# Dilated attention and a SiLU layer pair: dummy matmuls in TensorE's idle slots of the first batch, and a new order of the work

## The chip, the cores and the metric

The kernel runs on one core of a Trainium2 chip. The metric is the device time of one execution in microseconds; lower is better. The median of 13 runs of the kernel before is 312.4 us, from 310.62 to 316.19.

## The reference

Eight batches of eight heads, 576 positions of 64 numbers. In heads 0 to 3 a query sees the 32 positions up to its own; in heads 4 to 7 every fourth position of the last 128. The result of all heads, 512 numbers for each of 4608 tokens, goes through two matrix products with SiLU between them.

```python
scores = scale * np.matmul(q, k.transpose(0, 1, 3, 2))
mask_plain = (rel >= 0) & (rel < window)                                # window = 32
mask_dil = (rel >= 0) & (rel < window * dilation) & (rel % dilation == 0)   # dilation = 4
attn = np.exp(scores - max); attn = attn / (np.sum(attn) + 1e-09)
x = np.matmul(attn, v)            # to (tokens, 512)
h = x @ w_in                      # 512 x 2048
out = (h * (1.0 / (1.0 + np.exp(-h)))) @ w_out    # 2048 x 512
```

## The kernel before, in words

**Attention, per batch.** Plain heads are worked in six blocks of 96 queries (P steps), dilated heads by residue r modulo 4 in two halves of 72 queries (D steps, half ab). A score unit (S, L605) multiplies keys and queries of 64 rows each in two halves of the array (L632); ACT takes the exponential (L641, L645) and DVE multiplies by a mask (L650). In batch 0 the mask is added on TensorE instead by a matmul with the identity (L620). P and D steps multiply the probabilities by v with a column of ones (av, L677), and DVE divides by the sum (L680, L681) into oP or oD.

**Ways of q and k.** Batches 0 to 2 are loaded by POOL's queue into `nat` and transposed on TensorE: TD for dilated heads (L544, L557), TA and TB for plain heads (L521, L535, L582), TS and TR for the last rows of batch 0 (L594, L567). For batches 1 and 2 the N steps first pair the heads by copies (L652). Batches 3 to 7 are cast into DRAM by POOL's queue (`kq_s`, L141) and brought back by SP's transposing DMAs: two windows of the plain heads (L155), two of the dilated heads (L158).

**Ways of the result.** For batches 0 to 2 it is transposed on TensorE into xA (XP, L722; XD, L733). For batches 3 to 7 it is stored to DRAM in four parts, two of oP (L696) and two of oD (L715), and a transposing DMA (L450) brings each token group back as xA or xR when the four parts are stored.

**The two products.** Tokens are in ten groups: 256, 256 and then eight of 512, numbered 0 to 9. For each of 16 slices of 128 of the inner width, layer 1 (L892) makes h from x and w_in in four matmuls; ACT takes tanh (L901), DVE forms gT (L903). Layer 2 (L925) runs gT against w_out into y, in quarters of four matmuls; ACT copies y out and issues the store (L938, L939). Group 4 needs batch 3, group 5 batch 4, group 6 batch 5, group 7 batch 6.

**What sets the order.** The lists `order` (L743 to L767) give the sequence of a batch's steps, and a planner in Python (L280, L980 to L1037) merges them with the slices of layers 1 and 2 when the program is built. It keeps a clock of TensorE and the fill of ACT and DVE, gives each step a cost and a due time (`AT_DIL`, `AT_PLAIN` and the like are planned landings of loads), looks at the first LOOK attention steps and takes the first candidate that is ready and whose engines' backlog is under its limit. [...] PSUM banks are rings: h 2, y 1, s one of two banks, x 1, z 2; batch 0's small tiles may use x, z, h and y (L778).

**Loads.** POOL's queue issues q, k and v of batch 0 first (L205 to L209), then what ORDER (L56) lists: k0, r0 and v0 are the rest of batch 0, w0a to w3 parts of w_in, d1, p1, r1 and v1 dilated and plain q and k, raw v and shifted v of batch 1, o0 to o3 quarters of w_out. Batch 2 follows. The loads of batch b of 5 and more (`loads_gen`, L424) stand in POOL's queue behind small copies (`fence`, L427, L429) that wait for earlier transposing DMAs: of the batch before and of the group that needs batch b - 2.

**The start.** DVE clears a tile `warm` (L189, a part of vraw of batch 1) and eight matmuls of 512 columns from it into the y bank (L192) precede the first load's landing.

The planner's core, at the point that the change touches:

```python
        if pick is None:
            waits += [plan.heap[0][0]] if plan.heap else []
            plan.t = max(plan.t + 0.01, min(waits))
            continue
```

Of the kernel before, what the change touches and what calls it, by code (L numbers as in the profile page):

```python
# [16 lines left out]
def kernel(  # L17
# [35 lines left out]
    XR = 3  # L53
    NA = GA * GT
    BIG = 32768.0
    ORDER = "k0 r0 w0b v0 w0a w1 w2 w3 d1 p1 o0 r1 o1 o2 o3 v1".split()  # L56
    LOAD_US = {"w": 2.57, "o": 2.57, "d": 3.2, "p": 3.0, "r": 2.3, "v": 2.57, "k0": 2.2, "r0": 1.0, "v0": 2.3, "w0a": 1.3, "w0b": 1.3}
    AT_W0 = 11.4
    BIASED = (0,)

    cpool = ctx.enter_context(tc.tile_pool(name="const", bufs=1))
# [123 lines left out]
            )  # L185

    v_head = xRs[2][:, 0, : 2 * HN * D].bitcast(F32).rearrange("p (h d) -> p h d", h=HN)
    warm = vraws[1].rearrange("p a h r d -> p (a h r d)")
    nc.vector.memset(warm[:, :GT], 0.0)  # L189
    y_warm = ps_y.tile([P, GT], F32, tag="y", name="y_warm")  # L190
    for n in range(8):
        nc.tensor.matmul(y_warm, warm[:, :P], warm[:, :GT], start=True, stop=True)  # L192
    nc.vector.memset(warm[:, GT:], 0.0)
    nc.vector.memset(vraws[0], 0.0)
    nc.vector.memset(v_head[:W], 0.0)
    nc.vector.memset(ident_w[:, :W], 0.0)
# [161 lines left out]

    plan = Plan()
    t2 = at  # L360
    AT_DIL = {0: 6.1, 1: AT["d1"], 2: t2 + 7.0}
    AT_PLAIN = {0: 9.3, 1: AT["p1"], 2: t2 + 7.0}
    AT_VRAW = {0: 10.1, 1: AT["r1"], 2: t2 + 8.6}
    AT_VP = {0: 11.4, 1: AT["v1"], 2: t2 + 11.4}
    AT_CAST = t2 + 18.0
    AT_REST = AT["k0"]
    AT_V1 = AT["r0"]
    AT_VP1 = AT["v0"]
# [97 lines left out]
    def attention(b):  # L466
# [274 lines left out]

        if b == 0:
            order = [  # L743
                ("TA", 1, "q"), ("TA", 0, "q"), ("V", 0), ("TD", 3), ("TS", 1), ("TS", 0),
                ("TD", 0), ("TA", 0, "k"), ("TD", 2), ("TD", 1), ("TA", 1, "k"), ("S", 3),
                ("TR",), ("S", 4), ("S", 6), ("S", 0), ("S", 1), ("D", 0, 1), ("P", 1), ("S", 5),
                ("D", 0, 0), ("D", 0, 2), ("V", 1), ("P", 0), ("S", 2), ("P", 3), ("P", 2),
                ("D", 1, 1), ("P", 4), ("D", 0, 3), ("P", 5), ("XP", 0), ("XP", 1), ("D", 1, 2),
                ("XD", 0), ("D", 1, 0), ("XP", 4), ("D", 1, 3), ("XP", 5), ("XP", 2), ("XD", 1),
                ("XP", 3), ("M",), ("B",),  # L750
            ]
        elif pe_path:
            order = [
                ("N", "k"), ("TD", 3), ("TD", 0), ("TD", 2), ("V", 0), ("TD", 1), ("N", "rest"),
                ("TA", 1), ("N", "q"), ("S", 3), ("TA", 0), ("TB", 0), ("TB", 1), ("D", 0, 1),
                ("D", 0, 0), ("S", 4), ("D", 0, 2), ("S", 0), ("P", 1), ("S", 1), ("D", 0, 3),
                ("P", 2), ("P", 0), ("XP", 0), ("XP", 1), ("S", 5), ("S", 6), ("XD", 0), ("V", 1),
                ("D", 1, 3), ("XP", 2), ("S", 2), ("D", 1, 2), ("D", 1, 0), ("D", 1, 1), ("P", 3),
                ("XP", 3), ("P", 4), ("XD", 1), ("P", 5), ("XP", 4), ("XP", 5),
            ]  # L760
        else:
            order = [
                ("S", 2), ("S", 0), ("P", 1), ("S", 3), ("S", 4), ("S", 1), ("S", 5), ("P", 0),
                ("V", 0), ("P", 5), ("P", 3), ("D", 0, 3), ("V", 1), ("P", 4), ("P", 2),
                ("D", 1, 1), ("D", 1, 3), ("D", 0, 1), ("D", 0, 2), ("D", 1, 2), ("D", 1, 0),
                ("D", 0, 0),
            ]  # L767
            if pe_x:
                order.insert(order.index(("D", 0, 0)), ("XP", 0))
                order.insert(order.index(("D", 0, 0)), ("XP", 1))  # L770
                order.insert(order.index(("D", 0, 2)), ("XP", 2))
                order.insert(order.index(("D", 0, 2)), ("XP", 3))
                order.insert(order.index(("D", 1, 0)), ("XP", 4))
                order.insert(order.index(("D", 1, 0)), ("XP", 5))
                order += [("XD", 0), ("XD", 1)]
        for key in order:
# [3 lines left out]
            if kind == "N":  # L780
                st = Step(lambda ring, a=a: paired(*a), 0.0, (), [AT_PLAIN[b]], ("DVE",))
            elif kind == "B":
                st = Step(lambda ring: third_batch(), 0.0, (), [steps["XD", 1]], ())
            elif kind == "M":
                st = Step(lambda ring: masks_of(), 0.0, (), [steps["XD", 1]], ("DVE",))
            elif kind == "TA" and b == 0:
                st = Step(
                    lambda ring, a=a: trans_a0(ring, *a), 0.36, rings,
                    [AT_PLAIN[0]],
                )  # L790
            elif kind == "TD" and b == 0:
                st = Step(lambda ring, a=a: trans_d0(ring, *a), 0.17, rings, [AT_DIL[b]])
            elif kind == "TR":
                st = Step(lambda ring: trans_d1(ring), 0.34, rings, [AT_REST])
            elif kind == "TS":
                st = Step(lambda ring, a=a: trans_a1(ring, *a), 0.36, rings, [AT_REST])
            elif kind == "TA":
                st = Step(
                    lambda ring, a=a: trans_a(ring, *a), 0.36, rings,
                    [steps["N", "k"], steps["N", "rest"]], ("ACT",),  # L800
                )
            elif kind == "TB":
                st = Step(
                    lambda ring, a=a: trans_b(ring, *a), 0.18, rings, [steps["N", "q"]], ("ACT",)
                )
            elif kind == "TD":
                st = Step(lambda ring, a=a: trans_d(ring, *a), 0.28, rings, [AT_DIL[b]], ("DVE",))
            elif kind == "S":
                if not pe_path:
                    deps = [turned[b]]  # L810
                elif b == 0:
                    plain = [("TA", hp, nm) for hp in range(HP // 2) for nm in "kq"]
                    rest = [("TS", hp) for hp in range(HP // 2)]
                    dil = [("TD", h) for h in range(HN)]
                    keys = (plain, plain, plain + rest, dil, dil, dil + [("TR",)], dil + [("TR",)])
                    deps = [steps[key_] for key_ in keys[a[0]]]
                elif a[0] < 3:
                    deps = [steps[t, hp] for t in ("TA", "TB") for hp in range(HP // 2)]
                else:
                    deps = [steps["TD", h] for h in range(HN)]  # L820
                st = Step(
                    lambda ring, a=a: scores(ring, *a), 0.17 + 0.32 * (b in BIASED), ["s"] + (["hh"] if b < 2 else []),
                    deps + readers.get(base + a[0] - NP, []), ("ACT",) if b in BIASED else ("ACT", "DVE"),
                )
            elif kind == "V":
                st = Step(lambda ring, a=a: vd_of(*a), 0.0, (), [AT_V1 if b == 0 and a[0] else at_vraw], ())
            elif kind == "P":
                us = sorted({home["p", a[0], hp][0] for hp in range(HP // 2)})
                st = Step(
                    lambda ring, a=a: av_p(ring, *a), 0.13, rings,  # L830
                    [AT_VP1 if b == 0 and a[0] > 2 else at_vp] + [steps["S", u] for u in us],
                    ("DVE",),
                )
            elif kind == "D":
                us = sorted({home["d", a[0], a[1] // 2, h][0] for h in range(HN)})
                st = Step(
                    lambda ring, a=a: av_d(ring, *a), 0.13, rings,
                    [steps["V", a[0]]] + [steps["S", u] for u in us], ("DVE",),
                )
            elif kind == "XP":  # L840
                st = Step(lambda ring, a=a: x_p(ring, *a), 0.1, rings, [steps["P", a[0]]], x_eng)
            else:
                st = Step(
                    lambda ring, a=a: x_d(ring, *a), 0.28, rings,
                    [steps["D", a[0], r] for r in range(DIL)], x_eng,
                )
# [131 lines left out]
        l2 += [(g, st) for st in layer2(g, l1s_of[g])]  # L978

    plan.push(Step(None, 0.0), first_cast(), 0.0)  # L980
    LOOK = 8
    LIM_ATT = 1.1
    LIM_PAIR = 0.4
    LIM_L1 = 1.8
    SIDE = 0.9
    NEAR = 1.0
    SPARE = 6
    seconds = {st.mate for _, st in att if st.mate}
    side = 0.0
    while att or l1 or l2:  # L990
# [31 lines left out]
        if pick is None and g2 < SPARE and l2[0][1].rings and plan.backlog(l2[0][1].uses) <= 9.0:  # L1022
            l2[0][1].rings = ["y", "x", "z"]
            r = plan.ready(l2[0][1])
            if r is not None and r <= plan.t:
                pick = l2, l2[0]
        if pick is None:
            waits += [plan.heap[0][0]] if plan.heap else []
            plan.t = max(plan.t + 0.01, min(waits))
            continue  # L1030
# [37 lines left out]
```

The softmax here doesn't subtract the row's maximum and nothing guards it: scores larger than these inputs give would overflow.

## Time and profile before

| | |
|---|---|
| median of 13 runs | 312.4 us |
| the profiled execution, its own time | 313.16 us |
| its span, first to last instruction | 311.4 us |
| TensorE (PE) busy | 300.3 us, 96% |
| VectorE (DVE), ScalarE (ACT), GpSimd (POOL) busy | 196.4, 164.7, 54.7 us |
| PE busy in the first 23 us | 18.1 us |
| first h of layer 1 starts | 22.84 us |
| last layer 2 matmuls end | 308.0 us |

PE's row is matmuls, PEld's weight loads beside them. A timeline line gives start, length, engine, line, operation, tiles and count; in brackets stands idle time before it and what ended it. A line of waits gives who waited for whom, the total, the number of times and the longest. The issue of a DMA is shown at its engine's queue (SPq, ACTq), or at POOL; the data lands later. The chain of work that ended last lies 83% on PE, 36% in each of the two layers (L892, L925). From 23 us on PE is idle for little more than 6 us, 3.4 of them at the very end.

### The profile page before, as it was taken

To read this page: it belongs to the slowest core of one execution; us is meant where nothing else is said; L and a number is where in the kernel's file an instruction comes from. 1 tells how busy PE (TensorE), PEld (TensorE's weight loads), DVE (VectorE), ACT (ScalarE), POOL (GpSimd) and SP (SyncE) were. 2 spreads that over 40 slices of the span, in tenths; PEclk is the share of its full clock that TensorE was granted. 3 is DMA by queue.
4 is the path that set the end of the run, shared out by engine and by line. 5 is a ranking of instruction groups with operands and counts; after the bars stand their busy time and mean duration, and the time that the engine had idled before them with its cause. 6 is when DMAs were issued, how large, how long until landed. Compare 5 with 4: busy or idle time off the path is not lost.

```text
span 311.4 us, 6177 instructions
## 1 busy us (share of the span) xinstructions
PE 300.3 (96%) x2402; PEld 155.9 (50%) x2402; DVE 196.4 (63%) x498; ACT 164.7 (53%) x318; POOL 54.7 (18%) x86
## 2 busy tenths in 40 slices
PE   7789989999999999999999999998999999999995
PEld 3468855555445544554445444544454444444444
DVE  6389998699868735794589357944885255455000
ACT  7478873667673626444653456434644355355111
POOL 8854724000900005000500050000000000000000
PEclk9999999999999999999999999999999999999999
DMA  8999999999999749999999999964115400000122
GB/s 105 181 201 192 175 192 208 203 197 156 147 186 224 181 124 154 214 186 203 128 213 216 201 131 213 206 156 104 53 56 129 111 36 34 34 36 0 74 94 71
DMA packets 107382, 44.55 MB, mean 143 GB/s; under 512 B 73304, under 2 KB 102872, under 8 KB 107352
## 3 DMA queue, kind: packets, MB, share of 16 engines
q0 software_dynamic: 48528, 19.86, 52.4%
q1 hardware_dynamic: 53496, 14.91, 25.0%
q10 hardware_dynamic: 5328, 9.37, 8.9%
q8 instruction: 19, 0.31, 0.4%
q14 instruction: 11, 0.09, 0.1%
HBM read 39.81 MB, written 18.28 MB: 187 GB/s over the span
## 4 chain that ended last, share of the span: by engine, by line
PE 83%; DVE 6%; DMA 5%; ACT 3%; issue 1%; POOL 1%; SPq 0%; ACTq 0%; DVEq 0%; POOLq 0%
PE y L925 36%; PE h L892 36%; PE s L632 3%; PE av_d L677 3%; DMA nat<-in_q_dram 2%; PE av_p L677 2%; DMA xR<-x_s 2%; DVE gT L903 1%; DVE oD L681 1%; DVE probs L650 1%; DMA x_s<-oD 1%; PE s L620 1%; ACT probs L641 1%; ACT ob L938 1%; ACT kqD L510 1%
## 5 line engine op out<-in xcount | busy, mean ns | idle before, releaser
L925 PE MATMUL y<-w_out,gT 128*128 128x512 f16 (+1 forms) x592 | 137.8, 373 | 0.0
L901 ACT ACTIVATE th<-h 128x512 f32<-128x512 f32 (+1 forms) x160 | 88.9, 557 | 79.4 <-PE h L892 68.0
L903 DVE SCALAR_TENSOR_TENSOR gT<-th,h 128x512 f16<-128x512 f32 (+1 forms) x160 | 99.2, 629 | 47.7 <-ACT th L901 47.2
L892 PEld LDWEIGHTS <-w_in 128*128 128x128 f16 x640 | 59.0, 97 | 53.5 <-issue 2.5
L925 PEld LDWEIGHTS <-gT 128*128 128x128 f16 x592 | 55.1, 98 | 57.5
L892 PE MATMUL h<-xR,w_in 128*128 128x512 f16 x320 | 77.6, 379 | 1.1 <-DMA xR<-x_s 1.1
L892 PE MATMUL h<-xA,w_in 128*128 128x512 f16 (+1 forms) x320 | 62.1, 336 | 0.0
L938 ACT ACTIVATE ob<-y 128x512 f32<-128x512 f32 (+1 forms) x36 | 21.3, 591 | 42.7 <-PE y L925 42.7
L641 ACT ACTIVATE probs<-s 128x768 f16<-128x768 f32 (+2 forms) x32 | 24.7, 772 | 12.5 <-PE s L632 10.8
L677 PEld LDWEIGHTS <-probs 128*128 128x128 f16 x448 | 21.9, 98 | 16.4 <-DVE probs L650 3.4
L681 DVE TENSOR_TENSOR oD<-av_d,rcps 72x256 f16<-72x256 f32 x64 | 26.9, 421 | 2.2
L650 DVE TENSOR_TENSOR probs<-probs,mask_p 128x768 f16<-128x768 f16 x21 | 11.5, 552 | 22.5 <-ACT probs L641 22.5
L681 DVE TENSOR_TENSOR oP<-av_p,rcps 96x256 f16<-96x256 f32 x48 | 20.2, 421 | 1.6
L427 POOL COPY fence<-kqT 128x1 f16<-128x1 f16 x10 | 2.0, 211 | 94.3 <-DMA kqT<-kq_s 94.3
L645 ACT ACTIVATE probs<-s 128x384 f16<-128x384 f32 (+2 forms) x38 | 17.2, 479 | 1.1 <-PE s L632 1.1
L677 PE MATMUL av_d<-vd,probs 128*128 128x65 f16 x256 | 15.4, 196 | 1.3 <-DVE oD L681 0.6
L945 DVE TENSOR_SCALAR ob<-y 128x128 f32<-128x128 f32 x1 | 0.3, 292 | 20.6 <-ACT ob L943 20.6
L680 DVE RECIPROCAL rcps<-av_d 72x4 f32<-72x4 f32 x64 | 11.0, 172 | 2.7 <-PE av_d L677 2.7
L680 DVE RECIPROCAL rcps<-av_p 96x4 f32<-96x4 f32 x48 | 8.3, 172 | 6.5 <-PE av_p L677 6.5
L677 PE MATMUL av_p<-vp,probs 128*128 128x65 f16 x192 | 12.0, 194 | 0.3
L165 POOL DMA_DIRECT2D vraw<-in_v_dram x16 | 11.0, 692 | 5.5 <-DVE rcps L680 2.2
L650 DVE TENSOR_TENSOR probs<-probs,mask_d 128x576 f16<-128x576 f16 (+1 forms) x23 | 11.6, 512 | 0.0
(93 smaller groups left out, 157.4 us busy)
## 6 DMA issues: line engine op xcount, KB each, us to landing
out_dram<-ob ACTq DMA_DIRECT2D x35, 256.0 KB, 2.8
kq_s<-in_k_dram POOLq DMA_DIRECT2D x5, 576.0 KB, 9.6
kq_s<-in_q_dram POOLq DMA_DIRECT2D x5, 576.0 KB, 12.2
vp<-in_v_dram POOLq DMA_DIRECT2D x7, 384.0 KB, 8.1
w_out<-in_moe_w_out_dram POOLq DMA_DIRECT2D x4, 512.0 KB, 11.2
vraw<-in_v_dram POOLq DMA_DIRECT2D x8, 224.0 KB, 5.3
w_in<-in_moe_w_in_dram POOLq DMA_DIRECT2D x3, 512.0 KB, 9.8
x_s<-oP SPq DMA_DIRECT2D x10, 144.0 KB, 3.1
```

Source lines behind the costliest of these rows:

```text
L165: nc.gpsimd.dma_start(out=vraw[p0 : p0 + m1 - m0, ab].rearrange("p h r d -> p h (r d)"), in_=src[m0:m1],)
L641: nc.scalar.activation(p2, both[:, :, :n], AF.Exp, scale=scale)
L645: nc.scalar.activation(p2[:, i], sp[i][:, :n], AF.Exp, scale=scale)
L650: nc.vector.tensor_tensor(p2, p2, mk, ALU.mult)
L677: nc.tensor.matmul(a[:, i, : D + 1], lhs(i), rhs(i), start=True, stop=True)
L680: nc.vector.reciprocal(rcp[:n], a[:n, :, D : D + 1])
L681: nc.vector.tensor_tensor(o, a[:n, :, :D], rcp[:n, :, None].broadcast_to([n, HN, D]), ALU.mult)
L892: nc.tensor.matmul(h[:, :w], w_in16[:, c, f * P : (f + 1) * P], x_g[:, c], start=(c == 0), stop=(c == HP - 1),)
L901: nc.scalar.activation(th[:, :w], h[:, :w], AF.Tanh, scale=0.5)
L903: nc.vector.scalar_tensor_tensor(gTs[g][:, f, :w], th[:, :w], 1.0, h[:, :w], ALU.add, ALU.mult)
L925: nc.tensor.matmul(y, gTs[g][:, f, tb * P : (tb + 1) * P], w_out16[:, f, c0:c1], start=(f == 0), stop=(f == NFF - 1),)
L938: nc.scalar.activation(ob, y, AF.Copy, scale=0.5)
```

## The change

- The warming tile is now a part of kqD of batch 1, which no load writes; there are nine warming matmuls of 512 columns instead of eight.
- Where the planner finds no step ready before its time 18.0, and after 5.5, it puts a matmul of 128 columns from the warming tile into the y bank (a dummy). In the built program 75 of them stand among the steps of batch 0: 13 ahead of the first transposes (TD), 17 behind them, 45 between the later steps.
- The y ring is marked as taken until 18.0, so no step of batch 0 uses it before.
- ORDER, the load times and the planned landings are new: v0 moves ahead of r0, p1 ahead of all of w_in, w1 ahead of w0a, o1 ahead of o0.
- The three `order` lists and the planner's limits are new. The built program differs in the sequence of instructions on every engine; apart from the dummies and the ninth warming matmul TensorE runs the same matmuls. Four transposing steps of batch 1 (TA, TB) come ahead of the first layer 1 slice. In batches 3 to 7 the last steps are now a mix of D and P steps ending in P 1.

```diff
-    ORDER = "k0 r0 w0b v0 w0a w1 w2 w3 d1 p1 o0 r1 o1 o2 o3 v1".split()
-    AT_W0 = 11.4
+    ORDER = "k0 v0 r0 p1 w1 w0a w0b w2 w3 d1 r1 o1 o0 o2 o3 v1".split()
+    AT_W0 = 11.9
...
-    warm = vraws[1].rearrange("p a h r d -> p (a h r d)")
-    nc.vector.memset(warm[:, :GT], 0.0)
+    warm = kqDs[1].rearrange("p h r k m -> p (h r k m)")[:, :GT]
+    nc.vector.memset(warm, 0.0)
...
-    for n in range(8):
-        nc.tensor.matmul(y_warm, warm[:, :P], warm[:, :GT], start=True, stop=True)
-    nc.vector.memset(warm[:, GT:], 0.0)
+    for n in range(9):
+        nc.tensor.matmul(y_warm, warm[:, :P], warm, start=True, stop=True)
+    nc.vector.memset(vraws[1], 0.0)
...
-                ("S", 2), ("S", 0), ("P", 1), ("S", 3), ("S", 4), ("S", 1), ("S", 5), ("P", 0),
-                ("V", 0), ("P", 5), ("P", 3), ("D", 0, 3), ("V", 1), ("P", 4), ("P", 2),
-                ("D", 1, 1), ("D", 1, 3), ("D", 0, 1), ("D", 0, 2), ("D", 1, 2), ("D", 1, 0),
-                ("D", 0, 0),
+                ("S", 0), ("S", 2), ("S", 3), ("P", 5), ("S", 1), ("S", 4), ("V", 0), ("D", 0, 0),
+                ("P", 2), ("S", 5), ("V", 1), ("D", 0, 3), ("D", 1, 2), ("P", 3), ("D", 1, 0),
+                ("D", 0, 1), ("P", 4), ("D", 1, 3), ("P", 0), ("D", 1, 1), ("D", 0, 2), ("P", 1),
...
-    LOOK = 8
-    LIM_ATT = 1.1
-    LIM_PAIR = 0.4
-    LIM_L1 = 1.8
-    SIDE = 0.9
-    NEAR = 1.0
+    LOOK = 14
+    LIM_ATT = 1.0
+    LIM_PAIR = 1.2
+    LIM_L1 = 1.4
+    SIDE = 0.7
+    NEAR = 0.3
     SPARE = 6
+    WARM = 18.0
+    held = Step(None, 0.0)
+    held.done = WARM
+    plan.rings["y"].append(held)
...
         if pick is None:
+            if plan.t < WARM:
+                if 5.5 < plan.t:
+                    nc.tensor.matmul(
+                        y_warm[:, :P], warm[:, :P], warm[:, :P], start=True, stop=True
+                    )
+                plan.t += 0.056
+                continue
```

## The prediction

> **What bounds the kernel now.** I read the busy table first, then TensorE's (PE) timeline of the first 25 us, then its waits, then SyncE's (SP) queue where the one late wait ends.
>
> The first lines of the page: PE is busy 96% of the span, and the row of the granted clock is flat.
>
> ```profile
> PE 300.3 (96%) x2402; PEld 155.9 (50%) x2402; DVE 196.4 (63%) x498; ACT 164.7 (53%) x318; POOL 54.7 (18%) x86
> ...
> PEclk9999999999999999999999999999999999999999
> ```
>
> The timeline of PE (start, us of the piece) says otherwise for the beginning:
>
> ```profile
> 11.51 0.66 PE L620 MATMUL s<-mask_d,ident_w 128*128 128x288 f16 x2
> ...
> 15.60 0.85 PE L594 MATMUL ta<-ident_w,nat 96*64 96x96 f16 x16
> 16.38 0.52 PE L567 MATMUL td<-ident_w,nat 96*128 96x96 f16 x8
> ...
> 19.24 0.42 PE L620 MATMUL s<-mask_d,ident_w 128*128 128x288 f16 x2
> ...
> 22.84 1.91 PE L892 MATMUL h<-xA,w_in 128*128 128x256 f16 x16
> ```
>
> The same pair of mask matmuls takes 0.66 us at 11.51 and 0.42 at 19.24. PE runs at half clock until about 16.4, although eight warming matmuls stood at 1.20 to 4.79. So the clock row cannot be trusted here; durations can.
>
> Behind the first h, PE hardly waits. Its waits that matter:
>
> ```profile
> PE ta_q L582 <- DMA nat<-in_q_dram: 1.7, 1, 1.7
> ...
> PE h L892 <- DMA xR<-x_s: 1.1, 1, 1.1
> PE td L557 <- DMA nat<-in_q_dram: 0.6, 1, 0.6
> PE av_d L677 <- DVE oD L681: 0.6, 1, 0.6
> ```
>
> The 1.1 us is at 213.86, the first h of token group 7. SP's timeline ahead of it:
>
> ```profile
> 193.98 3.51 SPq L155 DMA_TRANSPOSE nat<-kq_s  x1
> 197.58 0.53 SPq L696 DMA_DIRECT2D x_s<-oP  x1
> 198.21 2.91 SPq L155 DMA_TRANSPOSE nat<-kq_s  x1
> 201.22 1.31 SPq L158 DMA_TRANSPOSE kqT<-kq_s  x1
> 202.65 0.85 SPq L715 DMA_DIRECT2D x_s<-oD  x1
> 203.60 1.44 SPq L158 DMA_TRANSPOSE kqT<-kq_s  x1
> 205.57 0.83 SPq L715 DMA_DIRECT2D x_s<-oD  x1
> 208.82 1.86 SPq L450 DMA_TRANSPOSE xR<-x_s  x1
> ```
>
> SP issues in order and each issue holds it for 0.3 to 3.5 us. The attention output's last store, ready when oD is written at 202.87, goes out at 205.57 behind a transposing load of the next batch (L158), and xR follows 3.25 us after it and lands 5.0 later. This SP queue, not a compute engine, is the second thing to watch.
>
> My yardstick is the **lag** of a point: clock time less the PE work that stands before it in program order, at full-clock durations (four matmuls of 512 columns 0.86 us, of 256 columns 0.44, a 96-column transpose 0.042, four av 0.12, a score unit 0.25 to 0.3, and about 0.1 for each change into or out of a score unit; masks and first transposes by their columns). Dummies count as no work. In the kernel before the lag is 12.7 at the first h (22.84, 10.1 of work), 14.45 at the first av_p of batch 1 (49.64), 14.8 at 60, still 14.6 at group 6 (180.44), 16.0 at group 7 (213.86, 197.8 of work) and 16.4 at the end. Both kernels hold 291.4 of such work, so the change of the lag at the end is the change of the time.
>
> [...] weight loads of L594 take 170 ns, those of L567 98; the eight warming matmuls were no sure cure. [...] xR holds SP 1.86 us and lands after 5.0. [...] The trace shows 175 to 208 GB/s in every slice from the second to the ninth (8 to 70 us), without a hole.
>
> **The change part by part.** *Dummies.* 75 of 128 columns and one more warming matmul. The warming ones are 0.43 apart, so a dummy is 0.11 at half clock, 0.054 at full: 4.0 to 8 us in all, meant for idle slots. The first 13 end at 1.2 + 9 x 0.43 + 13 x 0.11 = 6.5, where q lands at 6.18 now: 0.3 late. With the 16 transposes between (0.7 to 1.4) the next 17 end by 8.1 to 9.7, so the first scores start 0.7 to 2.3 us later than now (7.36). Cover: the second q half lands at 10.08 and vd's copy, which the first av needs, ends at 11.3. If the array stayed cold, the other 45 would cost 4.8 between 10 and 18, about 2 us after cover. I take them at nothing: 1.2 to 6.5 is then dense enough to get the clock early.
>
> *The clock.* From 10.08 to 16.4 PE ran without a break at half speed: 3.1 us could go. What is late next is the loads. p1 (576 KB) and w1 (512) now stand ahead of w0a, w0b (256) behind it. w0a lands at 12.52 + 6.2 = 18.7 now; the queue gives 512 KB per 2.5 us (w0a to w1), so 832 KB later is 22.8. The first h stays at about 22.9, with 1.3 us more work behind it (XD 1 and batch 1's TA and TB steps, whose p1 lands by 19: 13.5 for k0, then v0 1.3, r0 1.2, p1 3.0, and whose paired copies of 0.4 to 0.5 follow). Its lag: 22.9 - 11.4 = 11.5, a gain of 1.2 there.
>
> *The other loads.* Moving them swaps places, it doesn't shorten the queue. POOL issues them in 0.6 to 0.9 us each (v0's three and p1's four now pass the w loads), 6 to 15 us ahead of their landing, so its own time is covered. o0 now stands where o1 stood: behind the same set of loads, so 41.3 (30.9 + 10.4), with 27.7 of work before its first use: lag 13.6 at least. v1 is last in both:
>
> ```profile
> L178 POOL DMA_DIRECT2D vp<-in_v_dram x1: 1431/1431/1431, 34.0 to 34.0; - x1
> ...
> DMA to landing us min/median/max: 15.5/15.5/15.5
> ```
>
> It lands at 49.5, and 35.45 of work stands before its first reader: the lag cannot be under 14.15 there, against 14.45 now. Of the clock's 3.1 us some 0.3 is left, 0.6 if the 0.3 that PE waits near 60 goes too. VectorE, busy 16.1 of 17.0 us from 23 to 40, may spoil that. I take -0.4, bounds -0.6 and +0.5.
>
> *y kept for dummies.* The small tiles of batch 0 lose one of six PSUM slots until the planned 18 us. Nothing, hidden by the wait for w0a at 22.9; without that cover perhaps 0.5 (one copy of 0.42).
>
> *Search limits and the order of batches 3 to 7.* The number of changes into and out of score units is 70 in both. What moves is SP's queue. Now the P steps end some 7 us of PE work before the last D, so only the two oD stores are late. In the new order P 1, P 0 and the D's share the last 2 us: oD, oD and oP all come last. For batch 5 SP's order becomes L155, oP, L155, oD, L158, oD, L158, oP, xR, where now both oP go first and both oD stand ahead of the last L158. Counting from the first oP, whose last av step stands behind 149.9 of PE work: av, division and hand-over 0.95, oP 0.4, L155 2.5 (2.2 to 2.9), oD 0.95, L158 1.4, oD 0.95, L158 1.6, hand-over 0.4, last oP to xR 3.2, xR 4.7: 17.05. So xR lands at 166.95 of work plus lag, and group 6's first h is due at 165.8 plus lag: PE **waits 1.2** where it now waits nothing (its xR lands at 180.16, used at 180.44). Bounds 0 (shorter issues) and 1.9.
>
> For group 7 the pattern repeats from a start 1.2 later. The loads of batch 7 wait in POOL for group 6's xR; from that landing to the next it now takes 213.8 - 180.2 = 33.6, and PE has 31.2 of work between the two first h's. With one more store behind the last L158 the chain isn't shorter, so the wait would be 1.2 to 3.0; I take **2.4 for the 1.3 of now**, +1.1. Group 5 has one L158 less before the last oP: by the same sum xR comes about 1 us in time, nothing.
>
> *Sum.* -0.4 + 1.2 + 1.1 = +1.9. The profiled execution took 313.16 (311.4 span, 1.8 around it); it would be 315.1. It lies 0.8 above the median of the runs, 312.4; put on the median the forecast is 314.3.
>
> **Rivals.** *Same:* the ramp gives 0.4 and the late stores cost about as much: group 6 waits 0.6 and group 7 what it waits now, 312.4 - 0.4 + 0.6 = 312.6. For it: one wait takes up slack for the next. *Faster, by one mechanism:* SP's issues and landings fall on the short side of what the trace shows (L155 2.2, L158 1.35, store to xR 3.1, xR 4.2), so the sum of 17.05 becomes 15.5 and xR is in time at both groups. Then the 1.3 of now goes as well: 312.4 - 0.4 - 1.3 = 310.7. It decides below 15.9, the work between that av and the first h. For it: xR of group 5 took 4.2. Against it: at group 7 now, two stores and the L158s between them took their full 5.2 (201.2 to 206.4), and xR 5.0. *The dummies don't do it:* PE stays cold, the first av comes 2 us late, of which v1's load hides half; with the queue's +2.3 and no gain of the ramp, 312.4 + 2.3 + 1.0 = 315.7.
>
> **How the numbers follow.** Late stores 0.52 (314.3, own range 313.2 to 316.2), of which 0.08 ends under 314.0; cold dummies 0.04; same 0.25; faster 0.19. Slower by over 0.5%, about what a measurement of this kernel can tell from no change (1.6 us), is 0.48; within it 0.33; faster 0.19. The range 311.0 to 316.2 holds nearly all of the first three and leaves out most of the faster case. Its ends: -0.6 for the ramp and -0.8, over half of group 7's wait, for the low; +0.5, +1.9 and +1.4 (the three terms at or near their worst) for the high.
>
> **What would show it.** Clock: mask pairs of 0.42 us from about 8 on. Ramp: first h near 22.9, first av_p of batch 1 near 49.6 with lag 14.2. Queue: SP holding oD, L158, oD, L158, oP, xR in this order before groups 6 and 7, and PE waits on xR at both, 3.6 in sum. I am wrong if xR lands before both first h's, or if v1 lands well before 49 (then the ramp gains more).

## The result, and the profile after

The changed kernel takes 317.81 us (median of 11 runs, 314.56 to 320.75); the kernel before, measured beside it, 312.98 (48 runs). The ratio is 1.015, with a 95% interval of 1.012 to 1.018: slower, by 4.8 us, where the forecast was 1.9 slower and its range ended at 316.2. Here and below, a median is of all runs, while a ratio and its interval compare the faster runs alone, those within 1.5% of the fastest of each kernel. The profiled execution of the changed kernel is the longest of its twelve: 321.43 us, span 319.6.

The busy line of PE and the clock row on its page:

```profile
PE 307.2 (96%) x2478; PEld 160.7 (50%) x2478; DVE 195.8 (61%) x492; ACT 165.4 (52%) x323; POOL 54.1 (17%) x86
...
PEclk9987999999999999999999979997999999999999
```

PE is busy 6.9 us longer than before. The dummies' own busy time is 5.6 us, in part beside other matmuls. Apart from them and the ninth warming matmul the matmuls are the same, but some are slower: the clock row has dents that it had not before, at 16 to 32 us, 184 to 192 and 216 to 224 (8 us a digit). PE's waits:

```profile
PE h L892 <- DMA xR<-x_s: 4.9, 2, 3.0
...
PE ta L522 <- DVE pair_k L513: 0.9, 1, 0.9
```

The 1.1 us on xR of before has become 4.9, in two waits. The timeline of PE shows both, and the start (start, us, engine, line, tiles, count, idle time before):

```profile
7.89 0.41 PE L621 MATMUL s<-mask_d,ident_w 128*128 128x288 f16 x2
...
22.23 0.50 PE L522 MATMUL ta<-ident_w,pair_k 96*128 96x96 f16 x4 [0.92 <-DVE pair_k L513]
...
24.62 2.75 PE L892 MATMUL h<-xA,w_in 128*128 128x256 f16 x12
...
184.58 2.60 PE L892 MATMUL h<-xR,w_in 128*128 128x512 f16 x8 [2.96 <-DMA xR<-x_s]
...
219.56 3.42 PE L892 MATMUL h<-xR,w_in 128*128 128x512 f16 x8 [1.94 <-DMA xR<-x_s]
```

The mask pair takes 0.41 at 7.89: PE is at full clock 8 us sooner than before. The first h comes at 24.62, not sooner but later than before. The last two lines hold the surprise. Eight matmuls of 512 columns take 1.7 to 1.9 us at full clock (1.89 at 190.42); here they take 2.60 and 3.42. The stretches of the trace tell why (stretch, length, PE busy and count, granted clock, DMA share, GB/s):

```profile
185.60:189.00 3.40, 3.40 (x9) 0.50 0.85 102
189.00:219.70 30.70, 28.68 (x229) 1.00 1.04 182
219.70:223.10 3.40, 3.40 (x9) 0.51 0.00 0
```

After each of the two waits PE runs 3.4 us at half clock, which costs half of that, 1.7 us. So the wait of 3.0 is paid as 4.7.

SP's queue ahead of group 6, first in the kernel before:

```profile
164.10 0.32 SPq L696 DMA_DIRECT2D x_s<-oP  x1
164.52 4.82 SPq L155 DMA_TRANSPOSE nat<-kq_s  x2
169.57 0.85 SPq L715 DMA_DIRECT2D x_s<-oD  x1
170.54 1.33 SPq L158 DMA_TRANSPOSE kqT<-kq_s  x1
171.96 0.84 SPq L715 DMA_DIRECT2D x_s<-oD  x1
172.90 1.72 SPq L158 DMA_TRANSPOSE kqT<-kq_s  x1
175.52 1.84 SPq L450 DMA_TRANSPOSE xR<-x_s  x1
```

and in the changed kernel:

```profile
167.26 0.32 SPq L697 DMA_DIRECT2D x_s<-oP  x1
167.67 2.22 SPq L155 DMA_TRANSPOSE nat<-kq_s  x1
169.98 2.00 SPq L716 DMA_DIRECT2D x_s<-oD  x1
172.10 1.29 SPq L158 DMA_TRANSPOSE kqT<-kq_s  x1
173.48 0.85 SPq L716 DMA_DIRECT2D x_s<-oD  x1
174.44 1.62 SPq L158 DMA_TRANSPOSE kqT<-kq_s  x1
176.15 0.54 SPq L697 DMA_DIRECT2D x_s<-oP  x1
179.12 1.83 SPq L451 DMA_TRANSPOSE xR<-x_s  x1
```

This is the forecast's order, oP, L155, oD, L158, oD, L158, oP, xR. VectorE writes the last oP tile at 171.57; its store leaves at 176.15, 4.6 us later, because the rest of one oD store, a second one and two transposing loads stand ahead of it. Before, the last store left at 171.96 and only one transposing load followed it.

With the yardstick of the prediction (lag: clock time less PE work ahead at full clock), the 8.3 us between the two profiled executions lie here:

| place | lag before | lag after | difference grown since the row above |
|---|---|---|---|
| about 60 us | 14.8 | 15.3 | +0.5 |
| arrival at group 6 | 14.6 | 15.85 | +0.75 |
| first h of group 6 | 14.6 | 18.8 | +2.95, the wait |
| after the half clock there | 14.7 | 20.5 | +1.6 |
| first h of group 7 | 16.0 | 22.6 | +0.8, wait 1.94 for 1.11 |
| after the half clock there | 16.0 | 24.3 | +1.7 |
| end | 16.4 | 24.6 | -0.1 |

The +0.75 ahead of group 6 grew in small steps; its cause stays open.

### The profile page after: what moved, and what is told of

Read it like the earlier page. It is cut to its first block, busy times and chain, and to the rows that moved or that the text cites. A ratio compares the mean times of both kernels' runs of the same rounds, so it can differ in the third digit from the quotient of the medians.

```text
span 319.6 us, 6323 instructions
## 1 busy us (share of the span) xinstructions
PE 307.2 (96%) x2478; PEld 160.7 (50%) x2478; DVE 195.8 (61%) x492; ACT 165.4 (52%) x323; POOL 54.1 (17%) x86
## 4 chain that ended last, share of the span: by engine, by line
PE 75%; DMA 11%; DVE 7%; ACT 3%; issue 1%; SPq 1%; POOL 1%; ACTq 1%; POOLq 0%
PE h L892 32%; PE y L925 32%; DMA xR<-x_s 5%; DMA x_s<-oP 3%; PE s L633 3%; PE av_d L678 2%; DMA nat<-in_q_dram 2%; DVE gT L903 2%; PE av_p L678 2%; DVE oD L682 2%; ACT ob L938 1%; DMA kqT<-kq_s 1%; ACT probs L642 1%; DVE oP L682 1%; PE y_warm L1034 1%
## 5 line engine op out<-in xcount | busy, mean ns | idle before, releaser
L892 PEld LDWEIGHTS <-w_in 128*128 128x128 f16 x640 | 59.8, 99 | 57.7 <-issue 7.8
L925 PEld LDWEIGHTS <-gT 128*128 128x128 f16 x592 | 56.3, 98 | 61.2 <-issue 2.7
L892 PE MATMUL h<-xR,w_in 128*128 128x512 f16 x320 | 79.2, 387 | 5.0 <-DMA xR<-x_s 4.9
L892 PE MATMUL h<-xA,w_in 128*128 128x512 f16 (+1 forms) x320 | 64.3, 344 | 0.0
L642 ACT ACTIVATE probs<-s 128x768 f16<-128x768 f32 (+2 forms) x33 | 25.7, 780 | 12.6 <-PE s L633 10.4
L678 PEld LDWEIGHTS <-probs 128*128 128x128 f16 x448 | 21.2, 97 | 14.3 <-DVE probs L651 2.3
L651 DVE TENSOR_TENSOR probs<-probs,mask_p 128x768 f16<-128x768 f16 x21 | 11.6, 555 | 21.8 <-ACT probs L642 21.7
L646 ACT ACTIVATE probs<-s 128x288 f16<-128x288 f32 (+2 forms) x36 | 16.9, 478 | 0.0
L678 PE MATMUL av_d<-vd,probs 128*128 128x65 f16 x256 | 15.3, 193 | 0.0
L681 DVE RECIPROCAL rcps<-av_p 96x4 f32<-96x4 f32 x48 | 8.3, 173 | 10.6 <-PE av_p L678 10.5
L678 PE MATMUL av_p<-vp,probs 128*128 128x65 f16 x192 | 12.9, 194 | 0.3
L945 DVE TENSOR_SCALAR ob<-y 128x128 f32<-128x128 f32 x1 | 0.3, 292 | 20.6 <-ACT ob L943 20.6
```

What stands on the lines that cost most here:

```text
L642: nc.scalar.activation(p2, both[:, :, :n], AF.Exp, scale=scale)
L646: nc.scalar.activation(p2[:, i], sp[i][:, :n], AF.Exp, scale=scale)
L651: nc.vector.tensor_tensor(p2, p2, mk, ALU.mult)
L678: nc.tensor.matmul(a[:, i, : D + 1], lhs(i), rhs(i), start=True, stop=True)
L681: nc.vector.reciprocal(rcp[:n], a[:n, :, D : D + 1])
L892: nc.tensor.matmul(h[:, :w], w_in16[:, c, f * P : (f + 1) * P], x_g[:, c], start=(c == 0), stop=(c == HP - 1),)
```

## The experiments

Theory after the result: the new list of steps for batches 3 to 7 makes SP send the last store late, xR comes late, and each long wait (2.96 and 1.94 us) is followed by 3.4 us at half clock. Rivals: the ramp (dummies, order of loads, thin stretch at 20 us) is what costs; or the late xR comes from PE being earlier against a fixed cycle of loads, whatever SP's order. Experiments 1 to 4 ran on one chip (kernel before: 314.79), 5 to 8 on a second (313.29), 9 to 12 on a third (314.57). Ratios are to the kernel before on the same chip.

**1. The old list of steps put back into the changed kernel.**

```diff
-                ("S", 0), ("S", 2), ("S", 3), ("P", 5), ("S", 1), ("S", 4), ("V", 0), ("D", 0, 0),
+                ("S", 2), ("S", 0), ("P", 1), ("S", 3), ("S", 4), ("S", 1), ("S", 5), ("P", 0),
...
-                ("D", 0, 1), ("P", 4), ("D", 1, 3), ("P", 0), ("D", 1, 1), ("D", 0, 2), ("P", 1),
+                ("D", 1, 1), ("D", 1, 3), ("D", 0, 1), ("D", 0, 2), ("D", 1, 2), ("D", 1, 0),
+                ("D", 0, 0),
```

> The changed kernel with only the step list of batches 3 to 7 put back to the old one; loads, dummies, the lists of batches 0 to 2 and the planner's limits stay new. Theory (late stores of oP and oD in SP's queue make xR late at groups 6 and 7, and each such wait of PE over about 2 us also halves the clock for one window of 3.4 us): the waits for xR fall to at most 1.3 in sum, no halved window after 30 us, 313 to 314. Rival (the new start, dummies and loads, is what costs): stays at 317 to 318.

Measured 316.88 us, ratio 1.0106 (1.0037 to 1.0175). The wait at group 7 is gone, that at group 6 is 1.74 instead of 2.96, one of 1.11 appears at group 5, and one stretch of half clock follows (182.9 to 186.3). The forecast of 313 to 314 is not met: this kernel is still slower than the one before, and by its time alone it isn't clear of the changed kernel's 1.015. It reaches 59 us with a lag of 13.6, 1.2 better than before, and loses it as waits.

**2. Forty dummies ahead of the first h of groups 6 and 7.** They fill 2.2 us of each wait.

```diff
+            if f == 0 and g in (6, 7):
+                for n in range(40):
+                    nc.tensor.matmul(h[:, :P], ident, ident, start=True, stop=True)
```

> The changed kernel with 40 dummy matmuls of 128 columns ahead of the first slice of groups 6 and 7, so that PE is busy for the first 2.2 us of the wait for xR. Theory: xR still lands late, but the array keeps its full clock afterwards; each halved window of 3.4 us cost 1.7, so 2 to 3.5 us less: 314.5 to 316. Rival (the clock drops for another reason[...]): the halved windows stay and the time is 318 or up to 2 more.

Measured 318.23 us, ratio 1.016 (1.011 to 1.021). In the profiled execution (316.12, the fastest of its six) the clock is full from 6.8 us to the end, and 0.6 us of waiting on xR is left. Three of its six runs were granted the full clock throughout (a mean of 1.000), of the changed kernel's twelve one. So with PE's idle time at the two waits (2.96 and 1.94 without these dummies) filled, the 3.4 us at half clock behind each are gone. But the time did not follow: the median did not move, and the forecast of 314.5 to 316 is not met. That these dummies cost about what they save is likely, but not shown.

**3. No dummies** (the nine warming matmuls stay, y is still held).

```diff
-                if 5.5 < plan.t:
-                    nc.tensor.matmul(
-                        y_warm[:, :P], warm[:, :P], warm[:, :P], start=True, stop=True
-                    )
```

> The changed kernel without the 75 dummies; the nine warming matmuls, the held y bank and every order stay. Theory: loads set the end of the ramp, so 317 to 318.5, with PE at half clock for longer before 17. Rival (dummies save time in the ramp, and without them it would be worse): 319 or more. Rival (dummies delay real work): 316 or less.

Measured 319.85 us, ratio 1.018 (1.010 to 1.025), not to be told from the changed kernel (1.015). The 319.85 lies in the rival's "319 or more", but the kernel before, too, took 1.8 us longer on this chip than beside the changed kernel. The clock is half from 11.5 to 18.3 us, where with dummies it is full. Even so the lag at 59 us is 13.9, less than the 15.3 of the changed kernel's profile, and the end has 6.8 us of waits on xR. In this profile the ramp decides nothing at the end.

**4. The dummies alone in the kernel before** (75 dummies by the same rule, nine warming matmuls, the new warming tile, y held).

```diff
+    WARM = 18.0
+    held = Step(None, 0.0)
+    held.done = WARM
+    plan.rings["y"].append(held)
...
+            if plan.t < WARM:
+                if 5.5 < plan.t:
+                    nc.tensor.matmul(
+                        y_warm[:, :P], warm[:, :P], warm[:, :P], start=True, stop=True
+                    )
+                plan.t += 0.056
+                continue
```

> The kernel before with the dummies alone: warming tile in kqD, nine warming matmuls, y bank held until the planned 18 us, dummies in planned gaps; its own loads, lists and limits. Theory: the clock is full from about 5 on, the first h comes up to 1.5 earlier, but v1's landing at 49.5 keeps the gain under 0.6: 312 to 313. Rival (dummies cost): 314 or more. Rival (the half clock was worth its 3 us): 310 or less.

Measured 317.92 us in 22 scattered runs (311.92 to 321.0), ratio 1.002 (0.998 to 1.007). The two numbers disagree: the ratio leaves out 13 of these 22 runs, and 5 of the 27 of the kernel before, and the median of all runs is 3.1 us above that of the kernel before. So it isn't settled whether the dummies alone cost time; the forecast of 312 to 313 is not met. The start does gain: the first h comes at 20.32 instead of 22.84, with a lag of about 10.5 (estimated from the work ahead of it) instead of 12.7. At v1's first reader the lag is 14.23, against 14.45 before: v1 lands at 48.21, and its reader starts at 48.25. So v1's landing holds PE there. Later the profiled execution (320.94, one of the longest) waits 5.1 us for xR in three places, with one stretch of half clock.

**5. The changed kernel again, beside the next three.**

> The changed kernel unaltered, beside the next three on one chip. Theory (late xR and a clock halved by each long wait): again about 317 to 318 us, xR waits at groups 5 to 7 of 5 us or more in sum, and one or more stretches of half clock of 3.4 us. Rival (chance of one chip): below 315, without these.

Measured 319.61 us, ratio 1.018 (1.011 to 1.024). The profiled execution (320.3) waits 0.40, 3.48 and 1.59 us at groups 5, 6 and 7; the clock is half from 185.2, in the wait at group 6, to 188.6, and stays full at group 7. The result holds on another chip.

**6. Without the copy in POOL that holds the next loads until xR has landed.**

```diff
-        if b - 2 >= PEX:
-            nc.gpsimd.tensor_copy(fence[:, 2:3], x_of(first_of[b - 2])[:, HP - 1, GT - 1 :])
```

> The changed kernel without POOL's copy that makes the loads of batch b wait for the landing of xR of batch b-2 (L430); the loads still wait for the last transposing load of batch b-1 (L428). Theory (from group 5 on the cycle load, transposing load, store, xR is as long as PE's work for a batch, 31 to 34 us): kqT lands some 5 us before xR does (178.9 and 184.7 in the profile of the changed kernel), so the casts of batches 6 and 7 start 1 and then 5 us sooner, the transposing loads go out ahead of the last attention steps, xR of group 7 is in time, its wait of 1.9 and its halved clock (1.7) go: 317.8 becomes about 314. Rival (the order of SP's stores alone makes xR late): the stores keep their places behind the transposing loads, nothing changes at group 6, at most 1 at group 7: 317.

Measured 326.72 us, ratio 1.042 (1.035 to 1.048): 7 us slower than the unaltered kernel on the same chip. The theory's forecast is on the wrong side. Its waits, and the time from issue to landing of the xR loads:

```profile
PE h L890 <- DMA xR<-x_s: 8.1, 2, 6.5
PE h L890 <- DMA xA<-x_s: 4.2, 1, 4.2
```

```profile
DMA to landing us min/median/max: 5.4/6.9/8.5
```

In the changed kernel that line reads 5.2/5.3/5.4. xR of group 6, issued at 183.7, lands at 192.2. The loads of the next batch now run beside it: from 180 to 192 us the DMAs moved 176 GB/s, against 145 beside xR of group 6 in the changed kernel (179.12 to 184.54), which took 5.4. But in the kernel before xR of group 6 took 4.6 while they moved 195, so that these loads lengthen its way is an estimate, not shown. An earlier start of the loads is no gain by itself.

**7. Stores issued by ACT.**

```diff
-                nc.sync.dma_start(
+                nc.scalar.dma_start(
                     out=rows[:, j - 2 : j + 1],
...
-                nc.sync.dma_start(out=rows, in_=oD[:, ab].rearrange("p r h d -> p r (h d)"))
+                nc.scalar.dma_start(out=rows, in_=oD[:, ab].rearrange("p r h d -> p r (h d)"))
```

> The changed kernel with the attention outputs' stores (L697, L716) issued by ACT instead of SP; SP keeps the transposing loads, in the same order. Theory of the prediction (stores held up behind L158 in SP's queue): the last store of batches 5 and 6 leaves when its tile is ready, some 1 to 2 us sooner, and the wait at groups 6 and 7 falls by as much each, with the halved clock where it falls under 2: 314 to 315. Rival (the last oP is ready late in any case, or the cycle of loads is the bound): xR lands within 0.5 of where it did, 317 to 318; if ACT's own queue waits for VectorE at a store, h is held up and it is slower, 319.

Measured 319.52 us, ratio 1.020 (1.015 to 1.026): as the changed kernel, and as the rival's last part had it. PE no longer waits for xR at all, but this line is new:

```profile
PE h L892 <- DVE gT L903: 5.5, 7, 1.6
```

ACT works in order too. Two lines of its own waits show a tanh (th) held up until rcps and oP are there, which only the store ahead of it needs:

```profile
ACT th L901 <- DVE rcps L681: 1.8, 1, 1.8
ACT th L901 <- DVE oP L682: 1.7, 1, 1.7
```

So a store that isn't ready holds up the tanh behind it, then gT, then h, and PE loses about a microsecond in each of batches 3 to 7. The wait has changed its owner, and the time says nothing on SP.

**8. The new list of steps alone, in the kernel before.** The reverse of experiment 1:

```diff
-                ("S", 2), ("S", 0), ("P", 1), ("S", 3), ("S", 4), ("S", 1), ("S", 5), ("P", 0),
+                ("S", 0), ("S", 2), ("S", 3), ("P", 5), ("S", 1), ("S", 4), ("V", 0), ("D", 0, 0),
...
+                ("D", 0, 1), ("P", 4), ("D", 1, 3), ("P", 0), ("D", 1, 1), ("D", 0, 2), ("P", 1),
```

> The kernel before with nothing but the new list of steps for batches 3 to 7. Theory (with that list the last oP store is late): xR waits at groups 6 and 7 of 3 and 2 us in place of 0 and 1.1, a halved clock at each, 2 to 6 us more than the kernel before on this chip, 316 to 318. Rival (the list costs only because PE comes earlier in the changed kernel): waits under 2 in sum, within 1 us of before.

Measured 319.15 us, ratio 1.018 (1.013 to 1.024): this one list is worth the whole loss of the changed kernel on the same chip (1.018 in experiment 5). The waits on xR are 1.1, 0.6 and 3.1 at groups 5, 6 and 7, not 3 and 2 at 6 and 7 as expected; the long one is again followed by half clock:

```profile
213.13 1.04 PE L891 MATMUL h<-xR,w_in 128*128 128x512 f16 x4 [3.05 <-DMA xR<-x_s]
```

```profile
214.20:217.60 3.40, 3.40 (x23) 0.50 0.00 0
```

**9. Stores issued by POOL, in the changed kernel.** POOL stands idle between its casts and the next fence (for 20.6 us up to 175.8 in the changed kernel). All other engines keep their programs; SP has only transposing loads left.

```diff
-                nc.sync.dma_start(
+                nc.gpsimd.dma_start(
                     out=rows[:, j - 2 : j + 1],
...
-                nc.sync.dma_start(out=rows, in_=oD[:, ab].rearrange("p r h d -> p r (h d)"))
+                nc.gpsimd.dma_start(out=rows, in_=oD[:, ab].rearrange("p r h d -> p r (h d)"))
```

> The changed kernel with the attention outputs' stores (L697, L716) issued by POOL, which stands idle between the casts of batch b+1 and the fence of batch b+2; VectorE, ACT and PE keep their programs, SP keeps only transposing loads. Theory of the prediction (in SP's queue the stores and L158 hold each other up): L155 and L158 of batch 6 no longer wait behind a store that isn't ready, the stores leave when their tiles are ready, xR of group 6 is issued 1.5 to 3 us sooner (before 177.5 in the profile), the waits on xR come under 2 in sum and no clock is halved after 100 us: 317.8 becomes 313 to 314.5. Rival (the last oP itself is late, or POOL's issues take longer than SP's): xR within 0.7 of where it was, 316.5 to 318.5.

Measured 312.86 us (22 runs), ratio 0.998 (0.9955 to 1.0005). The loss is gone, as the theory said; the interval includes no change from the kernel before. SP's queue, and the last store in POOL's, ahead of group 6:

```profile
161.51 5.91 SPq L155 DMA_TRANSPOSE nat<-kq_s  x2
167.53 3.81 SPq L158 DMA_TRANSPOSE kqT<-kq_s  x2
175.50 2.20 SPq L451 DMA_TRANSPOSE xR<-x_s  x1
```

```profile
171.34 0.73 POOL L697 DMA_DIRECT2D x_s<-oP  x1
```

The last oP tile is written at 170.94 and its store leaves 0.4 us later, not 4.6; xR is issued at 175.50 instead of 179.12. PE waits for no xR, and the clock is full from 28.3 us on.

**10. Stores issued by POOL, in the kernel before.** Same diff.

> The kernel before with the same move of its stores to POOL. Theory (SP's queue makes xR of group 7 late there too, by 1.1 in the profile, more in some runs): the wait goes, 1 to 2 us less than before on the same chip, and fewer runs above 316. Rival (the loads' landing, not SP, sets it): within 0.7 of before.

Measured 313.04 us, ratio 0.9957 (0.9927 to 0.9987): 0.4% faster than the kernel before, the only version here whose interval lies under 1. It isn't shown to differ from experiment 9, whose median is 312.86. PE waits for no xR; above 316 us lie 1 of its 22 runs and 19 of the 59 of the kernel before. So SP's mixed queue cost a little there too.

**11. Twenty more dummies at the thin stretch of the ramp**, ahead of the transposes that waited 0.92 at 22.2.

```diff
+            if b == 1 and hp == 0:
+                cold = tps.rearrange("p a r m -> p (a r m)")[:, : 2 * P].bitcast(F32)
+                for n in range(20):
+                    nc.tensor.matmul(cold, ident, ident, start=True, stop=True)
```

> The changed kernel with 20 more dummies (128 columns, 1.1 us at full clock) ahead of batch 1's first transposes, where PE waited 0.92 for pair_k after waits of 0.27 and 0.29. Theory (the changed kernel's dummies end at 18 and this thin stretch lets the clock fall for 3.4 to 6.8 us): full clock from 8 to beyond 60, lag at the first h near 12.4, 13.3 at 45, and, since v1's landing at 49.3 sets a floor of 14.15 for the lag at its first reader, under 1 us of it left at 60; in the time 0 to 1 less than the changed kernel on this chip, and all the late waits unchanged. Rival (the ramp's loss passes through to the end): 2 to 3 less.

Measured 318.16 us, ratio 1.012 (1.006 to 1.018), not to be told from the changed kernel's 1.015, as the theory had it. The clock is full from 4.4 to 181.9 us and the lag at 59 is about 13.4, nearly 2 better than in the changed kernel's profile. PE then waits 2.3 and 2.2 on xR at groups 6 and 7. The ramp's gain is lost where it meets xR.

**12. Old list, stores on POOL and the twenty dummies together.**

> The changed kernel with before's list of steps for batches 3 to 7, the stores issued by POOL, and the 20 dummies ahead of batch 1's first transposes: ramp of the changed kernel kept warm, its late xR removed. Theory: no wait on xR over 1, full clock throughout, lag about 14.2 at v1 and 15 at the end against 16.4 before: 1 to 2 us faster than the kernel before on this chip, 311 to 312. Rival (the cycle of loads gives the gain back as waits whatever the queue): 313 to 315.

Measured 314.89 us, ratio 1.006 (1.002 to 1.009): the forecast of 311 to 312 failed, the rival's 313 to 315 holds. The clock is full from 5.6 us on, and still:

```profile
PE h L897 <- DMA xR<-x_s: 2.9, 2, 1.5
```

**What holds PE there.** POOL's copies behind xR mark its landings (here in the kernel before and in the changed one):

```profile
148.87 0.19 POOL L429 COPY fence<-xR 128x1 f16<-128x1 f16 x1 [2.01 <-DMA xR<-x_s]
...
180.28 0.19 POOL L429 COPY fence<-xR 128x1 f16<-128x1 f16 x1 [2.15 <-DMA xR<-x_s]
```

```profile
150.34 0.19 POOL L430 COPY fence<-xR 128x1 f16<-128x1 f16 x1 [2.72 <-DMA xR<-x_s]
...
184.65 0.19 POOL L430 COPY fence<-xR 128x1 f16<-128x1 f16 x1 [5.57 <-DMA xR<-x_s]
```

From one to the next it takes 31.4 us before, 34.3 after; 31.75 in experiment 9, 31.3 in 10, 31.6 in 12. From its first h of group 5 to that of group 6, less the wait for xR, PE needs 30.4 us before, 31.35 after, 31.3 in experiment 9, 30.45 in 10 and 30.1 in 12. So this cycle (landing of xR, loads, casts, transposing loads, stores, xR) is longer than PE's work in all five, by 0.4 to 3.0 us; in experiment 12 by 1.5, which is the wait at group 6. The new list in SP's mixed queue made it 2.9 us longer. Time that PE gains early comes back as a wait for xR (experiments 1, 11 and 12). No experiment made the cycle shorter than PE's work, so it is argued, not shown, that this would let the gain through.

## Why the prediction was wrong

The direction, the place and SP's order were right, the size was not.

- **Dummies at nothing, clock early:** right on the clock (0.41 from 7.89). In all ten profiles with the dummies it is full for the first time between 4.1 and 6.8 us; with the start of the kernel before it was full to stay only from 14.1, 16.4 and 19.6 us (experiment 10, before, experiment 8). That this saves time in the end is not shown: without the dummies the time can't be told apart (experiment 3).
- **First h at 22.9, lag 11.5:** wrong. w0a landed at 24.46, not 22.8, and the first h came at 24.62 with a lag of 13.35. The step reckoned 832 KB at the pace of w0a to w1; the queue was slower by 1.7 us, and by 0.3 to 1.4 in the nine other profiles with this order of loads.
- **The ramp's term, -0.4:** +0.5 in the profiled run, at its upper bound. The dummies end at 18, PE is busy for only 0.76 of the 2 us from 20 to 22, and the clock is half from 21.8 to 28.6, which no term foresaw. But the term isn't one number. In the seven profiles with this same start (after, experiments 1, 2, 5, 6, 7, 9) the first h of group 2, with equal work ahead, starts between 54.05 and 56.39 us, in the three with the start of before (before, 8, 10) between 54.65 and 55.68. The ramp's gain or loss is within that scatter.
- **v1's floor of 14.15:** half right. v1's landing does hold PE: in experiments 2, 3, 4, 5 and 12 its first reader starts 0.04 us after it. But v1 lands anywhere between 47.8 and 50.8 us in the 14 profiles, so in experiments 1, 2, 3, 6, 11 and 12 the lag there is 12.6 to 13.6, less than the forecast called possible. (The forecast's own 49.5 less 35.45 is 14.05.)
- **y held for dummies, nothing:** no run shows a PE wait for it; not measured alone.
- **SP's order and late xR at groups 6 and 7:** right, and the cause of the loss: the list brings the loss (experiment 8), stores taken out of SP's queue remove it (experiment 9). Group 7 waited 1.94 where 2.4 was forecast; the "1.3 of now" was 1.11 in the line that the forecast shows.
- **Nothing for group 5:** right in the changed kernel (0.10, and 0.40 in experiment 5), but experiments 1 and 8 have 1.1 there.
- **The first failed step is the size of the wait at group 6:** 1.2 forecast, 1.9 at most; 2.96 measured, 3.14 in experiment 3 and 3.48 on the second chip (experiment 5). From the first oP store to the landing of xR the step had 16.1; it took 17.2. The first oD held SP for 2.1 instead of 0.95, and xR took 5.4 from issue to landing, not 4.7. The first oP store itself left at 167.26, and not at 166.7 (149.9 of work, a lag of 15.85 on arrival, 0.95), 0.6 later than reckoned; 1.2 + 1.1 + 0.6 is the 2.9 measured.
- **The second failed step is the sum:** it priced a wait at its length. In the profiled pair each of the two was followed by 3.4 us at half clock, +3.3 us in all, and no term stood for it. The forecast had seen that PE begins at half clock, yet treated the clock as settled once full.

How much of the median's 4.8 us each of the two is can only be estimated, since the profiled run is the longest. Experiment 5's profile (320.3, near its median of 319.6) has 5.5 us of waits for xR against 1.1 before, and one stretch of half clock, 1.7. And each run's mean granted clock is on record: (1 - clock) x span, the time that half clock cost in it, the ramp included, is 7.4 us in the profiled run but 3.4 on average over the twelve, and 2.0 over the 22 runs of experiment 9, which has the same start and is about 5 us faster (on another chip). By this estimate waiting is the larger part, and half clock in the late waits about 1.4 us.

Of the rivals, "faster" assumed that SP's issues fall on the short side; the first oD store did the contrary. Its short times add up to 15.85, not 15.5, so it had 0.05 us to spare against its 15.9. "Same" needed 0.6 at group 6. "Cold dummies" had the wrong mechanism; that its 315.7 is the nearest number is chance.

These stay open: why in experiment 1 xR lands about a microsecond later than before with the old list; and whether, with the stores on POOL, a ramp without the thin stretch (or without dummies) would end sooner, which no run here measures.

## What to carry to other kernels

A store that isn't ready yet, in an in-order queue that also issues the next batch's loads, holds them up and is held up by them (the first oD store held SP for 2.0 us here, and the last oP store left 4.6 us after its tile was written): compare the time a tile is written with the time its store leaves, and put stores into a queue whose engine stands idle, not one with compute behind it (ratio 0.998 with POOL, 1.020 with ACT). Before speeding up a start, measure the DMA cycle that later feeds the array; if it is as long as the array's work (31.4 us against 30.4 in the kernel before), the gain comes back as a wait, as it did here. Price a wait of 2 to 3 us of TensorE at its length plus the half clock that may follow (3.4 us here, which cost 1.7).

## What the runs showed of the hardware

- **Half clock after most waits of 1.7 us and more.** All twelve runs and both kernels together have 23 waits of PE of 1.1 us or more between 60 and 300 us. Of those from 2.30 us up (to 6.5) all eight brought half clock, in the wait or within 1.1 us of its end (for 3.41 us, once 6.83, at the wait of 6.5). Of the six between 1.7 and 2.3, two were followed by it; of the nine under 1.7, none. No sharp limit shows: 1.74 did it once and 2.29 once did not.
- **Thin work may end the full clock too.** With PE busy for 0.76 of 2 us, in short transposes and av's, the clock fell for 6.83 us in the changed kernel, and not at all in experiment 2 (stretch, length, PE busy and count, granted clock, DMA share, GB/s):

```profile
20.00:22.00 2.00, 0.76 (x12) 0.94 1.30 187
22.00:24.00 2.00, 1.77 (x23) 0.50 1.35 187
```

```profile
20.00:22.00 2.00, 0.76 (x13) 1.00 1.38 196
22.00:24.00 2.00, 1.84 (x36) 1.00 1.39 204
```

Of the seven profiles with this stretch (0.76 to 0.89 busy) five show half clock behind it, for 3.41 or 6.83 us; experiments 2 and 5 don't. With the stretch filled (experiments 11 and 12, 1.51 and 1.67 busy) the clock stays full, but two runs can't prove that the filling did it.

- **A plain store needn't go by SP.** On POOL it held its queue for 0.73 us, and xR was issued 4.2 us after the last store's start against 3.0 with SP; 1.2 us slower, yet 3.6 us earlier in all. So what else stood in the queue mattered more here than the time from store to xR.
